# Moving low-part subtractions to GpSimd and reordering the entrance and the change of stages in a fused attention and MLP kernel

## The chip, the cores and the metric

One core of a Trainium2 chip runs the whole program. The metric is the time of one execution on the device in microseconds (us), as the median of several runs. Engines: TensorE (PE), VectorE (DVE), ScalarE (ACT), GpSimd (POOL) and SyncE (SP), whose queue issues the transfers.

## What is computed

```python
def _attn_ref(q, k, v, mem_k, mem_v):
    ...
    for c in range(nc):
        ...
        scores = scale * np.matmul(q_c, k_full.transpose(0, 1, 3, 2))
        ...
        out[:, :, c_start:c_end] = np.matmul(a, v_full)

def _moe_ref(x, w_in, w_out, g_ln):
    h = x @ w_in
    ...
    solu = h * sm
    ...
    ln = (solu - mu) / np.sqrt(var + 1e-06) * g_ln
    return (ln @ w_out).astype(np.float32)

def _moe2_ref(x, w_in, w_out):
    h = x @ w_in
    relu6 = np.clip(h + 3.0, 0.0, 6.0)
    g = h * relu6 / 6.0
    return (g @ w_out).astype(np.float32)

def reference(**kwargs):
    ...
    x = np.ascontiguousarray(attn_out.transpose(0, 2, 1, 3)).reshape(B * S, H * D)
    x = _moe_ref(x=x, **moe_kwargs)
    return _moe2_ref(x=x, **moe2_kwargs)
```

The attention is chunked (chunks of 32 queries, 16 keys to the left, 8 to the right, 8 memory keys; 4 x 8 heads of 768 x 64). x is 3072 x 512; the first MLP goes over 1024 (softmax gate, norm, `g_ln`), the second over 2048. The weights are converted to float32 and split in the kernel.

## The kernel before

The 24 tiles of 128 tokens go through attention, the first MLP's two products (`m1`, `m2`) and its norm in a loop (`BODY`). The result x2, 512 x 3072, goes to DRAM. Then follow two further stages, which are what the change is about.

**Third stage** (`mm`, L839): the product with the second MLP's `w_in`, in 6 blocks of 512 tokens and 8 units of 256 columns each, 48 units n = 8 b + u. A 2 x 2 block product is done with 7 products (the matrices' quarters are summed beforehand), and each product runs as three passes over a high and a low part of each operand: 7 x 2 x 3 = 42 matmuls of 128 x 256 a unit. VectorE puts the 7 products together (`o1` to `o4`, L866 to L878), ScalarE copies one (`p1`) and applies relu (L881), VectorE clips (`clip`, L884), and SP stores the unit to DRAM (`g_store`).

**Last stage** (`g4`, L929): the product with `w_out`, 12 groups of 256 tokens by 8 steps, again 7 products of three passes, 21 matmuls a step. A step's operand is loaded (`g_load`), summed (four `g_sum`, L914, VectorE) and split (`g_hi`, `g_lo`).

**Splitting.** Every operand tile of 128 x 512 is made into a high part (`hi_of`, L740, ScalarE) and a low part (`lo_of`, L743, VectorE: the raw tile minus the high part). There are 28 tiles of the third stage's weights (`load_w`, `w_hi`, `w_lo`; four raw tiles, halves of `qb` and `pb`), 28 of the last stage's (`load_b`, `b_hi`, `b_lo`; raw tiles `xo0`, `xo1`), of which 8 are made early, stored and fetched back (`STAGED`, `store_b`, `fetch_b`), and 7 a block of the activations (`x_hi`, `x_lo`), with four sums on GpSimd (`x_sum`, L810).

**What sets the order.** The framework keeps the order in which the program is written on each engine. Around the two stretches this is: `LAST` (L88), a table of steps for the end of the second stage, with the weights 0 to 17 prepared between the pieces of `m2`; then a loop over the units, `unit` (L1213), which spreads the rest of the weights (two a unit in units 0 to 4) and the last stage's (`b_jobs`: two a unit from unit 40 on, then one a step); and the loop over the steps (L1301), whose `get_ready` prepares the operand three steps ahead.

The core of a unit, as far as a sentence cannot say it:

```python
emit("o1", n); tail(n - 1, 0); emit("o2", n); tail(n - 1, 1); emit("o3", n)
emit("relu", n, 0); emit("p1", n + 1); low(jobs[:1])
emit("o4", n); emit("relu", n, 1); low(jobs[1:])
```

(The lines are joined here; `tail` is `clip` and, at its second call, `g_store`.)

Of the kernel before, what the change touches and what calls it, by code (L numbers as in the profile page):

```python
# [87 lines left out]
LAST = """  # L88
    m2:6,8 m2_e:6,2 m2_s:6,2 m2:6,9 m2:6,10 ln_p:23,0 ln_h:23,0 ln_l:23,0 m2:6,11 m2_e:6,3 m2_s:6,3 ln_p:23,1 ln_h:23,1
    ln_l:23,1 x_sum:0,1 x_sum:0,2 x_hi:0,5 x_lo:0,5 x_hi:0,3 x_lo:0,3 x_sum:0,4 x_hi:0,2 x_lo:0,2 x_sum:0,3  # L90
    w_hi:0 w_lo:0 load_w:4 m2:7,0 w_hi:1 w_lo:1 load_w:5 m2:7,1 w_hi:2 w_lo:2 load_w:6 m2:7,2 m2_e:7,0 m2_s:7,0 x_hi:0,6
    x_lo:0,6 x_hi:0,4 x_lo:0,4 w_hi:3 w_lo:3 load_w:7 w_hi:4 w_lo:4 load_w:8 m2:7,3 w_hi:5 w_lo:5 load_w:9 m2:7,4
    w_hi:6 w_lo:6 load_w:10 m2:7,5 m2_e:7,1 m2_s:7,1 w_hi:7 w_lo:7 load_w:11 w_hi:8 w_lo:8 load_w:12 m2:7,6 w_hi:9 w_lo:9 load_w:13
    m2:7,7 w_hi:10 w_lo:10 load_w:14 m2:7,8 m2_e:7,2 m2_s:7,2 w_hi:11 w_lo:11 load_w:15 w_hi:12 w_lo:12 load_w:16 m2:7,9
    w_hi:13 w_lo:13 load_w:17 m2:7,10 w_hi:14 w_lo:14 load_w:18 m2:7,11 m2_e:7,3 m2_s:7,3 w_hi:15 w_lo:15 load_w:19
    w_hi:16 w_lo:16 load_w:20 w_hi:17 w_lo:17 load_w:21
# [4 lines left out]
def tile_chunked_attention_solu_hardswish(  # L101
# [863 lines left out]
    with tc.manual_schedule():  # L965
# [228 lines left out]
        for entry in LAST.split():  # L1194
            run(entry)

        def tail(n, k):
            if n >= 0:
                emit("clip", n, k)
                if k:  # L1200
                    emit("g_store", n)

        b_jobs = {}
        for k, n in enumerate(STAGED):
            b_jobs[NU + NU * (k // 2) + 6 * (k % 2)] = [("b", n)]
        for n in range(11):
            b_jobs.setdefault(NU * (NX - 1) + n // 2, []).append(("b", n, 1))
        for k, n in enumerate((11, 12, 13, 18, 19, 20, 25, 26, 27)):
            b_jobs[NX * NU + k] = [("b", n, 1)]
        order = [j for n in sorted(b_jobs) for j in b_jobs[n]]  # L1210
        following = {a: b for a, b in zip(order, order[2:])}

        def unit(n, jobs):  # L1213
# [21 lines left out]
            low(late)
            if n + 1 < NX * NU:
                emit("mm", n + 1)
            i = n - NX * NU + 2
            if i == 1:
                get_ready(None, 0)  # L1240
# [11 lines left out]
            low(jobs[1:])
            if i in (-1, 0):
                get_ready(i + 1, None)
            if i == 1:
                get_ready(2, 1)
# [101 lines left out]
```

## Time and profile before

| | |
|---|---|
| median of 3 runs | 887.65 us (886.84 to 889.75) |
| the profiled execution, own time | 888.17 us |
| its span, first to last instruction | 886.4 us |
| mean granted TensorE clock | 0.994 of full |
| TensorE busy | 865.3 us (98%) |
| VectorE busy | 757.9 us (86%) |
| ScalarE busy | 467.0 us (53%) |
| GpSimd busy | 225.9 us (25%) |
| the chain that ended last | TensorE 77%, VectorE 10%, DMA 6% |

The span is that of the execution that the profiler recorded; its own time is 1.8 us longer, for what lies around the first and the last instruction. Shares are means over stages with different limits; a stretch is judged by its own rows.

### The profile page before, as it was taken

Reading aid. Unit: us, or ns where it says so; the run is one execution under the profiler, and the core shown is the slowest. Engines: PE = TensorE matmul, PEld = TensorE weight load, DVE = VectorE, ACT = ScalarE, POOL = GpSimd, SP = SyncE. Lnnn points to the kernel's source line nnn. Section 1 sums busy time; section 2 is a strip of 40 time slices with the busy share of each in tenths; the row PEclk is TensorE's granted clock in tenths of the full one; section 3 lists DMA queues with packets and bytes.
Section 4 is the critical chain, followed back from the end, with each engine's and each line's share of the span. In section 5 each row is a group of like instructions: output and inputs, shape, how many; then the busy total and the mean of one; then the engine's idle time right before and its main releaser. Section 6 shows DMA issues by size and latency. Waiting matters only on the chain.

```text
span 886.4 us, 20093 instructions
## 1 busy us (share of the span) xinstructions
PE 865.3 (98%) x7523; PEld 815.5 (92%) x7523; DVE 757.9 (86%) x1621; ACT 467.0 (53%) x865; POOL 225.9 (25%) x205
## 2 busy tenths in 40 slices
PE   9989999999999999999999999999999999999997
PEld 7777899899998989899999999999989999999997
DVE  6889987878778788677999989898899998989996
ACT  5777636566564655445545454455555444444442
POOL 4327624546455556340121111110000000000000
PEclk9999999999999999999999999999989999999999
DMA  8894347879896997438553645535786443444442
GB/s 230 213 222 113 82 128 226 237 227 300 246 269 202 290 266 230 160 121 248 194 195 147 219 153 205 195 139 209 258 268 214 147 142 122 143 139 138 142 142 73
DMA packets 184013, 168.26 MB, mean 190 GB/s; under 512 B 107116, under 2 KB 154220, under 8 KB 183916
## 3 DMA queue, kind: packets, MB, share of 16 engines
q1 hardware_dynamic: 183916, 166.98, 61.0%
q8 instruction: 59, 0.97, 0.4%
q14 instruction: 38, 0.31, 0.1%
HBM read 108.22 MB, written 58.72 MB: 188 GB/s over the span
## 4 chain that ended last, share of the span: by engine, by line
PE 77%; DVE 10%; DMA 6%; issue 3%; ACT 2%; SPq 2%; POOL 0%; DVEq 0%; ACTq 0%; POOLq 0%
PE acc L935 22%; PE acc L846 20%; PE h L556 12%; PE m L641 12%; PE tp L613 2%; PE tp L525 2%; PE sc L469 2%; DMA q_raw<-in_q_dram 1%; DMA f_pb<-sums 1%; DMA f_xo<-sums 1%; PE tp L456 1%; PE tp L507 1%; PE idle L988 1%; DMA f_xo<-w2d 1%; PE tp L441 1%
## 5 line engine op out<-in xcount | busy, mean ns | idle before, releaser
L641 PE MATMUL m<-lnh,wo 128*128 128x384 f32 x512 | 138.7, 344 | 0.0
L881 ACT ACTIVATE f_s<-f_e,constants 128x512 f32<-128x512 f32 x96 | 69.3, 722 | 96.1 <-DVE f_e L874 87.0
L556 PE MATMUL h<-w,xh 128*128 128x512 f32 x336 | 106.2, 397 | 0.1
L641 PEld LDWEIGHTS m<-lnh,wo 128*128 128x128 f32 x512 | 91.7, 189 | 0.3
L641 PE MATMUL m<-lnl,wo 128*128 128x384 f32 x256 | 88.4, 345 | 0.0
L556 PEld LDWEIGHTS h<-w,xh 128*128 128x128 f32 x336 | 61.0, 188 | 11.6 <-ACT lnh L284 0.3
L258 POOL TENSOR_SCALAR w2t<-w2t 128x512 f32<-128x512 f32 x30 | 58.4, 1946 | 51.7 <-ACT w2t L251 51.7
L884 DVE SCALAR_TENSOR_TENSOR f_s<-f_s,f_e 128x512 f32<-128x512 f32 x96 | 70.7, 737 | 0.0
L556 PE MATMUL h<-w,xl 128*128 128x512 f32 x168 | 65.7, 391 | 0.0
L245 ACT ACTIVATE kT<-tp 128x448 f32<-128x448 f32 (+3 forms) x61 | 24.7, 458 | 57.3 <-PE tp L441 49.9
L641 PEld LDWEIGHTS m<-lnl,wo 128*128 128x128 f32 x256 | 48.3, 189 | 0.0
L740 ACT ACTIVATE b_e<-f_z 128x384 fp32r<-128x384 f32 (+1 forms) x48 | 27.4, 575 | 30.0 <-DVE f_z L914 12.3
L740 ACT ACTIVATE b_qb<-f_kn 128x384 fp32r<-128x384 f32 (+1 forms) x48 | 27.1, 570 | 28.1 <-DVE f_kn L914 19.9
L245 ACT ACTIVATE qb<-tp 64x512 f32<-64x512 f32 x48 | 28.5, 594 | 18.7 <-PE tp L456 18.3
L571 ACT ACTIVATE e<-h,lst 128x1024 f32<-128x1024 f32 x24 | 26.5, 1104 | 22.2 <-DVE lst L565 22.2
L556 PEld LDWEIGHTS h<-w,xl 128*128 128x128 f32 x168 | 31.5, 188 | 6.9
L740 ACT ACTIVATE b_km<-f_q 128x384 fp32r<-128x384 f32 (+1 forms) x48 | 27.2, 570 | 19.3 <-DVE f_q L914 16.7
L878 DVE TENSOR_TENSOR f_e<-acc,f_e 128x512 f32<-128x512 f32 x48 | 32.9, 685 | 1.2
L288 DVE TENSOR_TENSOR lnl<-tp,lnh 128x512 fp32r<-128x512 f32 x41 | 26.7, 686 | 7.8 <-ACT lnh L284 7.8
L740 ACT ACTIVATE b_v<-f_xl 128x512 fp32r<-128x512 f32 x24 | 15.2, 632 | 34.4 <-DVE f_xl L914 33.6
L870 DVE TENSOR_TENSOR f_e<-acc,f_e 128x512 f32<-128x512 f32 x48 | 32.8, 683 | 0.1
L565 DVE TENSOR_REDUCE lst<-h 128x1 f32<-128x1024 f32 x24 | 29.2, 1217 | 3.5 <-PE h L556 3.4
(451 smaller groups left out, 2577.3 us busy)
## 6 DMA issues: line engine op xcount, KB each, us to landing
g<-f_s SPq DMA_DIRECT2D x48, 512.0 KB
v<-in_v_dram SPq DMA_DIRECT2D x176, 56.0 KB
w2raw<-in_moe_w_out_dram SPq DMA_DIRECT2D x16, 512.0 KB
w2raw<-in_moe_w_in_dram SPq DMA_DIRECT2D x16, 512.0 KB
w2d<-w2t SPq DMA_DIRECT2D x32, 256.0 KB
pair<-w2d SPq DMA_DIRECT2D x16, 512.0 KB
sums<-sums SPq DMA_DIRECT2D x16, 512.0 KB
q_raw<-in_q_dram SPq DMA_DIRECT2D x24, 256.0 KB
```

What stands on the lines that cost most here:

```text
L245: ACT.activation(out=out, in_=in_, func=AF.Copy)
L258: ENG[eng].tensor_scalar(out=tf, in0=tf, scalar1=U_LO, scalar2=U_HI, op0=ALU.max, op1=ALU.min)
L556: PE.matmul(h[:, f], a[:, kt], w[kt][:, f * 512:(f + 1) * 512], start=n == 0, stop=n == 3 * NKT - 1)
L565: DVE.tensor_reduce(st_t[i][:, 2:3], h_t[i].rearrange("p a b -> p (a b)"), axis=AX.X, op=ALU.max, negate=True)
L641: PE.matmul(acc, w[fc // 2][:, fc % 2, dc * P:(dc + 1) * P], a[:, fc], start=n == 0, stop=n == len(todo) - 1)
L740: ACT.activation(out=hl[0], in_=r, func=AF.Copy)
L846: PE.matmul(o, w[wl][:, c * P:(c + 1) * P], x[xl][:, c], start=m == 0 and half == 0, stop=m == 5, skip_group_check=True)
L870: DVE.tensor_tensor(c_of(n)[1], bank(n % 2, 2), wide(c_of(n)[0][:, 1]), ALU.add)
L878: DVE.tensor_tensor(c, bank(n % 2, 3), c, ALU.add)
L881: ACT.activation(out=g_of(n)[k], in_=c_of(n)[k], func=AF.Relu, bias=three, scale=1.0)
L884: DVE.scalar_tensor_tensor(out=g_of(n)[k], in0=g_of(n)[k], scalar=6.0, in1=c_of(n)[k], op0=ALU.min, op1=ALU.mult)
L935: PE.matmul(bank(t % 2, k)[:, half], g[al][:, G_BLOCK[p]], b_op[j, p][bl], start=j == 0 and m == 0 and half == 0, stop=j == NU - 1 and m = ...
```

## The change

`lo_of`, `w_lo` and `b_lo` get the engine as an argument, and 13 `w_lo` and 15 `b_lo` in the two stretches run on GpSimd. The end of the second stage and the units 0 to 9 stand in one explicit list, `LAST`; the units 39 to 47 and the steps 0 to 22 in another, `CHANGE`. In `LAST` the activations' first sum and its high part come first, and `mm:0` stands ahead of the last four pieces of `m2`. In `CHANGE` the steps run 0, 2, 1, 4, 3, 6, 5, 8, 7 and so on to 14, 13, 15. The raw tiles of `load_b` become four for 12 of the loads (two halves of `v0` beside `xo0` and `xo1`), the last stage's sums use two buffers in place of four, and the activations' homes are written out. Units 10 to 38 keep the order they had (`head`, `body`), and so do the steps from 23 on.

```diff
-    def lo_of(hl, r):
-        DVE.tensor_tensor(hl[1], r, hl[0].bitcast(F32), ALU.subtract)
+    def lo_of(hl, r, eng=DVE):
+        eng.tensor_tensor(hl[1], r, hl[0].bitcast(F32), ALU.subtract)
...
-    def w_lo(n):
+    def w_lo(n, eng=DVE):
         hl = w_halves(*W_HOME[BLOCKWISE[n]])
-        lo_of(hl, w_raw(n))
+        lo_of(hl, w_raw(n), eng)
...
+    B_RAW = ["xo0", "xo1"] * 4 + ["xo0", "xo1", "v0", "v0+"] * 3 + ["xo0", "xo1"] * 4
...
-    def b_lo(n, straight=0):
+    def b_lo(n, straight=0, eng=DVE):
         hl = b_dst(n, straight)
-        lo_of(hl, b_raw(n))
+        lo_of(hl, b_raw(n), eng)
...
-    G_RAW = (("xh", 0), ("kn0", 0), ("q0", 0), ("z1", 0))
-    G_SUM = (("xl", 0), ("kn1", 0), ("q1", 0), ("z1", 512))
-    G_HL = (("v0", "v1", 32, 0), ("qb", "pb", 32, 0), ("km", "kT", 16, 48), ("e0", "e1", 32, 0))
+    G_RAW, G_SUM = ("xh", "kn0", "pe", "z1"), ("xl", "kn1")
+    G_HL = (("km", "kT", 16, 48), ("qb", "pb", 32, 0), ("v0", "v1", 32, 0), ("e0", "e1", 32, 0))
...
 LAST = """
...
+    load_w:6 x_hi:0,4 m2:7,4 m2_s:7,0 m2:7,5 w_lo:4 x_lo:0,6 load_w:7 w_hi:6 x_lo:0,5 w_hi:5 m2_s:6,3 w_lo:6,pool
+    w_lo:5 load_w:8 m2:7,6 load_w:10 w_hi:7 m2:7,7 w_hi:8 x_lo:0,4 mm:0 p1:0 o1:0 load_w:9 w_lo:7,pool w_hi:10 w_hi:9
...
+CHANGE = """
...
+    b_lo:13,1,pool g4:0 load_b:19 g_lo:2,0 g_hi:1,1 g_load:6 o3:47 g_lo:2,1 g_lo:1,1 relu:46,0 g_hi:4,0 relu:46,1
...
+        for entry in LAST.split():
+            run(entry)
+        body(9)
+        for n in range(10, 39):
+            head(n)
+            body(n)
+        for entry in CHANGE.split():
+            run(entry)
         drains = []
-        for i, (t, j) in enumerate(G_SEQ):
-            emit("g4", i)
...
+        for i, (t, j) in list(enumerate(G_SEQ))[23:]:
+            if i > 23:
+                emit("g4", i)
             if i + 5 < len(G_SEQ):
                 emit("g_load", i + 5)
-            if i in (2, 4, 6, 8):
-                emit("fetch_b", 20 + i // 2)
...
+            get_ready(i + 3, i + 2)
```

Where the rows stand now. GpSimd from the end of the second stage on, before: the norm's last power and the first block's four sums of the activations (`f_v` is their raw tile, `f_pe` and `f_pn` the sums).

```order
L601 TENSOR_TENSOR lst<-lst,constants 128x1
L810 TENSOR_TENSOR f_pe<-f_v_4902 128x512
L810 TENSOR_TENSOR f_pn<-f_v_4904,f_pe 128x512
L810 TENSOR_TENSOR f_pe<-f_v_4904,f_pn 128x512
L810 TENSOR_TENSOR f_pn<-f_v_4904,f_v_4902 128x512
L810 TENSOR_TENSOR f_xh<-f_v_4902 128x512
L810 TENSOR_TENSOR f_xl<-f_v_4904,f_xh 128x512
```

GpSimd at the same place in the change (`b_wb`, `b_lh`, `b_wa` and so on are the weights' homes, `f_qb` and `f_pb` raw tiles):

```order
L654 TENSOR_TENSOR lst<-lst,constants 128x1
L865 TENSOR_TENSOR f_pe<-f_v_4902 128x512
L796 TENSOR_TENSOR b_wb_5085<-f_qb,b_wb_5085 128x512
L865 TENSOR_TENSOR f_pn<-f_v_4904,f_pe 128x512
L865 TENSOR_TENSOR f_pe<-f_v_4904,f_pn 128x512
L865 TENSOR_TENSOR f_pn<-f_v_4904,f_v_4902 128x512
L796 TENSOR_TENSOR b_wb_5141<-f_qb,b_wb_5141 128x512
L796 TENSOR_TENSOR b_lh_5208<-f_pb,b_lh_5208 128x512
L796 TENSOR_TENSOR b_lh_5208<-f_qb,b_lh_5208 128x512
L796 TENSOR_TENSOR b_wa_5109<-f_qb,b_wa_5109 128x512
L796 TENSOR_TENSOR b_x2r<-f_pb,b_x2r 128x512
L796 TENSOR_TENSOR b_ll_5294<-f_pb,b_ll_5294 128x512
```

One low part now stands between the first and the second sum, and twelve more follow where nothing stood.

GpSimd from the last of the activations' sums on, in the change; before, nothing follows that sum:

```order
L865 TENSOR_TENSOR f_xl<-f_v_4904,f_xh 128x512
L865 TENSOR_TENSOR f_xh<-f_v_4904,f_xl 128x512
L865 TENSOR_TENSOR f_xl<-f_v_4904,f_v_4902 128x512
L796 TENSOR_TENSOR b_wb_5085<-f_xo_5697,b_wb_5085 128x512
L796 TENSOR_TENSOR b_wb_5085<-f_xo_5808,b_wb_5085 128x512
L796 TENSOR_TENSOR b_wb_5085<-f_v_4902,b_wb_5085 128x512
L796 TENSOR_TENSOR b_wb_5141<-f_xo_5697,b_wb_5141 128x512
L796 TENSOR_TENSOR b_wo<-f_v_4902,b_wo 128x512
L796 TENSOR_TENSOR b_wb_5141<-f_xo_5808,b_wb_5141 128x512
L796 TENSOR_TENSOR b_lh_5208<-f_xo_5697,b_lh_5208 128x512
```

The low parts of the last stage's weights stand there, one after the other, 15 in all; `f_xo` and `f_v` are their raw tiles.

VectorE in the last unit of the third stage, before: `o1` to `o4` are the rows out of `acc`, L884 the clips of the unit before, L914 and L743 the sums and low parts of a step's operand.

```order
L867 TENSOR_TENSOR f_e_5456<-acc,f_pe 128x512
L884 SCALAR_TENSOR_TENSOR f_s_5402<-f_s_5402,f_e_5398 128x2x256
L870 TENSOR_TENSOR f_e_5456<-acc,f_e_5456 128x512
L884 SCALAR_TENSOR_TENSOR f_s_5402<-f_s_5402,f_e_5398 128x512
L874 TENSOR_TENSOR f_e_5456<-acc,f_e_5456 128x256
L878 TENSOR_TENSOR f_e_5456<-acc,f_e_5456 128x512
L914 TENSOR_TENSOR f_q_8040<-f_q_7840 128x128 x2
L914 TENSOR_TENSOR f_q_8040<-f_q_8040,f_q_7840 128x128
L743 TENSOR_TENSOR b_pb<-f_kn_7780,b_qb 128x384
L914 TENSOR_TENSOR f_q_8040<-f_q_7840,f_q_8040 128x128
L743 TENSOR_TENSOR b_pb<-f_kn_8020,b_qb 128x512
```

VectorE at the same place in the change (the four rows out of `acc` into `f_e_5390` are this unit's; L969 are the sums, L796 the low parts):

```order
L924 TENSOR_TENSOR f_e_5390<-acc,f_pe 128x512
L931 TENSOR_TENSOR f_e_5268<-acc,f_e_5268 128x256
L935 TENSOR_TENSOR f_e_5268<-acc,f_e_5268 128x512
L927 TENSOR_TENSOR f_e_5390<-acc,f_e_5390 128x512
L969 TENSOR_TENSOR f_xl<-f_pe 128x128
L796 TENSOR_TENSOR b_v_8043<-f_pe,b_v_8042 128x384
L931 TENSOR_TENSOR f_e_5390<-acc,f_e_5390 128x256
L796 TENSOR_TENSOR b_v_8043<-f_xl,b_v_8042 128x512
L796 TENSOR_TENSOR b_pb<-f_kn_7613,b_qb 128x512
L969 TENSOR_TENSOR f_xl<-f_xh 128x128
L969 TENSOR_TENSOR f_xl<-f_xl,f_xh 128x128
L935 TENSOR_TENSOR f_e_5390<-acc,f_e_5390 128x512
```

No clip stands there any more, and sums and low parts of three steps stand among the unit's four operations.

TensorE where the third stage begins, before: the last rows of the second stage (`m`) and the first of `mm:0`.

```order
L641 MATMUL m_5252<-lnl,wo 128x384
L641 MATMUL m_5252<-lnh,wo 128x384 x2
L641 MATMUL m_5252<-lnl,wo 128x384
L641 MATMUL m_5252<-lnh,wo 128x384
L846 MATMUL acc<-b_kn_5029,b_wb_5117 128x256
L846 MATMUL acc<-b_kn_5030,b_wb_5117 128x256
```

TensorE in the change: the last rows of `mm:0` and what follows it.

```order
L903 MATMUL acc<-b_t_5133,b_wb_5085 128x256
L903 MATMUL acc<-b_t_5132,b_wb_5085 128x256
L903 MATMUL acc<-b_z_5143,b_wa_5109 128x256 x6
L694 MATMUL m_5276<-lnh,wo 128x384
L694 MATMUL m_5276<-lnl,wo 128x384
L694 MATMUL m_5276<-lnh,wo 128x384 x2
```

Four pieces of the second stage, 32 matmuls, stand behind `mm:0` now.

## Rows read from the trace of the kernel before

**Rows 1.** Windows: length, busy us (instructions) per engine, PEclk (granted clock), DMA share, GB/s.
```profile
400.00:410.00 10.00, 10.00 (x69) 9.88 (x67) 5.90 (x10) 4.62 (x8) 0.00 (x0) 1.00 0.82 241
430.00:440.00 10.00, 9.96 (x84) 9.58 (x83) 10.00 (x18) 6.30 (x13) 0.00 (x0) 1.00 0.42 153
480.00:600.00 120.00, 120.00 (x1061) 120.00 (x1060) 108.55 (x184) 58.03 (x106) 17.84 (x13) 1.00 0.50 181
642.60:651.00 8.40, 7.08 (x35) 6.51 (x36) 8.30 (x19) 3.82 (x7) 0.00 (x0) 0.60 0.70 237
700.00:880.00 180.00, 179.77 (x1580) 179.18 (x1580) 161.81 (x480) 81.02 (x157) 0.00 (x0) 1.00 0.42 134
```

**Rows 2.** Timeline of TensorE, entrance: start, us, line, tiles, matmuls, [idle before <-releaser].
```profile
387.87 0.63 PE L613 MATMUL tp<-ident,so 128*128 128x128 f32 x4 [1.01 <-DVE so L606]
...
406.89 0.87 PE L846 MATMUL acc<-b_kn,b_wb 128*128 128x256 f32 x6
...
453.28 0.84 PE L846 MATMUL acc<-b_q,b_wb 128*128 128x256 f32 x6
453.96 0.84 PE L846 MATMUL acc<-b_km,b_wa 128*128 128x256 f32 x6
454.64 2.88 PE L846 MATMUL acc<-b_wo,b_wb 128*128 128x256 f32 x24
```

**Rows 3.** Timeline of TensorE, change of the two stages.
```profile
640.28 0.39 PE L935 MATMUL acc<-b_wb,b_v 128*128 128x256 f32 x2
642.56 2.81 PE L935 MATMUL acc<-b_wb,b_v 128*128 128x256 f32 x16 [1.90 <-DVE b_v L743]
...
647.77 0.58 PE L935 MATMUL acc<-b_wb,b_pb 128*128 128x256 f32 x1 [1.32 <-DVE b_pb L743]
...
651.68 0.39 PE L935 MATMUL acc<-b_wb,b_km 128*128 128x256 f32 x2
...
689.67 1.35 PE L935 MATMUL acc<-b_wb,b_v 128*128 128x256 f32 x9 [0.87 <-DVE f_s L946]
...
691.20 0.39 PE L935 MATMUL acc<-b_wb,b_qb 128*128 128x256 f32 x2
```

**Rows 4.** Timeline of GpSimd, same columns: sums of the activations.
```profile
384.22 1.62 POOL L810 TENSOR_TENSOR f_pn<-f_v,f_pe 128x512 f32<-128x512 f32 x1
...
424.44 1.62 POOL L810 TENSOR_TENSOR f_xl<-f_v,f_xh 128x512 f32<-128x512 f32 x1
```

**Rows 5.** Timeline of VectorE beside and away from these.
```profile
384.62 1.78 DVE L743 TENSOR_TENSOR b_q<-f_v,b_q 128x512 fp32r<-128x512 f32 x1
...
399.09 0.68 DVE L743 TENSOR_TENSOR b_wa<-f_pb,b_wa 128x512 fp32r<-128x512 f32 x1
...
424.84 0.68 DVE L878 TENSOR_TENSOR f_e<-acc,f_e 128x512 f32<-128x512 f32 x1
```

**Rows 6.** Timeline of VectorE: pace back to back, and the last unit's o4.
```profile
434.07 0.41 DVE L874 TENSOR_TENSOR f_e<-acc,f_e 128x256 f32<-128x256 f32 x1
434.41 0.68 DVE L743 TENSOR_TENSOR b_wo<-f_qb,b_wo 128x512 fp32r<-128x512 f32 x1
435.01 0.68 DVE L878 TENSOR_TENSOR f_e<-acc,f_e 128x512 f32<-128x512 f32 x1
...
645.95 0.69 DVE L878 TENSOR_TENSOR f_e<-acc,f_e 128x512 f32<-128x512 f32 x1
...
654.72 0.49 DVE L914 TENSOR_TENSOR f_kn<-f_kn 128x128 f32<-128x128 f32 x2
...
656.64 0.69 DVE L743 TENSOR_TENSOR b_ll<-f_xo,b_ll 128x512 fp32r<-128x512 f32 x1
```

**Rows 7.** Groups of VectorE from 453 to 640: busy us, mean ns | idle before.
```profile
L884 DVE SCALAR_TENSOR_TENSOR f_s<-f_s,f_e 128x512 f32<-128x512 f32 x80 | 58.9, 737 | 0.0
```

**Rows 8.** Chain of waits at the entrance: start, us, what.
```profile
396.92 2.81 DMA f_pb<-sums
...
406.23 3.99 DMA f_pb<-sums
```

More of the change, by code (lines that the diff above doesn't have):

```diff
@@ L88 @@
 LAST = """
[L89 to L93, printed above, removed]
@@ new lines @@
+    w_lo:23 load_w:24 o1:4 o2:4 clip:3,0 load_w:25 w_hi:24 w_hi:25 w_lo:24 o3:4 load_w:27 p1:5 w_hi:27 o1:5 clip:3,1
+    o4:4 x_hi:1,3 w_lo:22,pool load_w:26 o2:5 g_store:2 w_hi:26 x_lo:1,3 mm:6 p1:6 w_lo:26 x_hi:1,2 o3:5 o4:5
+    w_lo:25,pool load_b:14 w_lo:27,pool relu:4,0 relu:4,1 clip:4,0 clip:4,1 x_lo:1,1 x_lo:1,2 o1:6 o2:6 o3:6 x_sum:1,4
+    x_sum:1,3 mm:7 p1:7 x_hi:1,5 x_lo:1,5 x_hi:1,4 x_lo:1,4 o4:6 x_hi:1,6 x_lo:1,6 mm:8 g_store:3 relu:5,0 relu:5,1
+    clip:5,0 clip:5,1 load_b:15 g_store:4 load_x:2 relu:6,0 o1:7 relu:6,1 p1:8 o2:7 o3:7 o4:7 mm:9 p1:9 clip:6,0 o1:8
@@ L812, in x_hl @@
     def x_hl(b, i):
-        return [t.rearrange("p (k t) -> p k t", k=2) for t in halves(*X_HOME[(7 * b + i) % len(X_HOME)])]
+        tag = X_HOME[b][i]
+        where = ("wo", int(tag[2]), 16) if tag[:2] == "wo" else ((tag + "0", tag + "1"),) if tag in ("kn", "q", "t") else (tag,)
+        return [t.rearrange("p (k t) -> p k t", k=2) for t in halves(*where)]
     def x_hi(b, i):
@@ L898, in g_tile @@
     def g_tile(i, which):
-        tag, o = which[i % 4]
-        return home(tag, F32)[:, o:o + 512].rearrange("p (b t) -> p b t", t=P)
+        return home(which[i % len(which)], F32)[:, 0:512].rearrange("p (b t) -> p b t", t=P)
     def g_hl(i):
@@ L1192, in emit, with head @@
             run(name + ":" + ",".join(map(str, args)))
[L1194 to L1213, printed above, removed]
+        def head(n):
             b, u = divmod(n, NU)
-            late = []
             if b + 1 < NX:
@@ L1235, in unit, with taken_over @@
[L1235 to L1240, printed above, removed]
+            for kind, *a in taken_over(n) + jobs(n):
+                emit(kind + "_hi", *a)
+            for kind, *a in taken_over(n):
+                emit(kind + "_lo", *a)
+            emit("mm", n + 1)
+        def taken_over(n):
+            b, u = divmod(n, NU)
+            return [("x", b + 1, i) for i in (4, 5, 6)] if u == 7 else []
@@ L1246, in unit @@
             emit("relu", n, 0)
-            if n + 1 < NX * NU:
-                emit("p1", n + 1)
-            low(jobs[:1])
+            emit("p1", n + 1)
+            for kind, *a in jobs(n)[:1]:
+                emit(kind + "_lo", *a)
             emit("o4", n)
             emit("relu", n, 1)
[L1252 to L1256, printed above, removed]
-            for job in mine:
-                if job in following:
-                    emit("load_b", following[job][1])
-                if len(job) == 2:
-                    emit("store_b", job[1])
@@ L1262, in unit @@
-            if b + 1 < NX and u in (4, 5):
+            for kind, *a in jobs(n)[1:]:
+                emit(kind + "_lo", *a)
+            for kind, *a in jobs(n):
+                if kind == "b":
+                    emit("load_b", B_ORDER[B_ORDER.index(a[0]) + 2])
+                    emit("store_b", *a)
+            if u in (4, 5):
                 emit("x_sum", b + 1, 8 - u)
```

116 lines of the change are left out of this document (64 added, 52 removed).

## The prediction

> **What bounds the kernel now.** I read the windows of busy time first, to find the stretches in which TensorE is not full. In long stretches it is: 120.00 of 120 us between 480 and 600, 179.77 of 180 between 700 and 880 [rows 1]. There nothing can be won by moving work between other engines. What is left are the two stretches that the change rewrites, and there I read TensorE's timeline against its own pace. At full clock a product of six matmuls starts 0.68 us after the one before (453.28 to 453.96), so a unit of third-stage work (`mm`, seven products) takes 4.76 us and a step of the last stage (`g4`, 21 matmuls) half of that, 2.38 us [rows 2].
>
> The entrance: `mm:0` starts at 406.89, `mm:9` at 454.64. That is 47.75 us for nine units that need 9 x 4.76 = 42.84, so 4.9 us are lost. Ahead of it TensorE waits 1.01 us at 387.87 for the `so` tile of VectorE [rows 2]. Together 5.9 us.
>
> The change of stages: `g4:0` starts at 640.28 and the 18th step at 691.20. 50.92 us for 17 steps that need 40.46: 10.5 us are lost [rows 3]. Of these 1.90, 1.32 and 0.87 are waits for VectorE (642.56, 647.77, 689.67). The rest of the stretch from 642.56 to 651.68 holds 40 matmuls, 4.53 us at pace, and takes 9.12; without the 1.32 of waiting that is 3.3 us too many, and the granted clock there is 0.60 of the full 2.4 GHz, most of it at the 1.2 GHz level [rows 1, 3]. It fell after the wait of 1.90 us; after those of 1.01 and 0.87 us it did not [rows 2, 3]. The remaining 3.1 us are small waits for VectorE.
>
> So at most 16.4 us can be won, 1.8% of the time, all of it on the path: TensorE's lost time is the program's.
>
> **The change, part by part.** The work is the same, matmul for matmul; what moves are the orders, and 13 `w_lo` and 15 `b_lo` from VectorE to GpSimd.
>
> *VectorE's load.* Back to back, a 512-element operation there costs 0.60 us and the 256-element one 0.34 (434.07, 434.41, 435.01), and getting one `g4` step ready (four sums of about 0.20, two low parts of 0.47 and 0.60) 1.92 (654.72 to 656.64) [rows 6]. So a unit (`o1` to `o4`, two clips) costs 5 x 0.60 + 0.34 = 3.34 of its 4.76 us, and a last-stage step 1.92 of 2.38. Before, units 40 to 45 carried two `b_lo` each but the last (4.54 us), and steps 0 to 8 one each (2.52, over TensorE's 2.38): this is why VectorE came late at 640 and stayed late. The 15 moved `b_lo` take 15 x 0.60 = 9.0 us off it in this stretch, and the 13 `w_lo` 7.8 us off the entrance.
>
> Adding the durations in the new order, with 1.2 us for two of the three activations' low parts ahead of `mm:40` as still running when it starts: by the end of `mm:47`, 38.1 us later, VectorE has 32.5 us of work to do (42 operations of 0.60, 8 of 0.34, 12 of 0.20, 2 of 0.47, and the 1.2); by `g4:9`, at 61.9, it has 56.8; by `g4:13`, at 71.4, 66.9. The spare is 5.6, 5.1 and 4.5 us; I take the smallest. In the entrance 49.7 us of VectorE work stand before `mm:10` at 70.7: a spare of 21 us.
>
> *What GpSimd takes back.* The cover of the moved subtractions is a GpSimd that stood idle; its 15 need at most 15 x 1.62 = 24.3 us of the 40 they have. They are not free. While GpSimd subtracted for 1.62 us at 384.22, a VectorE subtraction between two SBUF tiles took 1.78 us (384.62) and not 0.68 (399.09); one that reads PSUM kept its 0.68 (424.84) beside the GpSimd operation of 424.44 [rows 4, 5]. The worst price is thus 1.10 us of VectorE time for each moved operation. The least: between 453 and 640 the 80 clips average 737 ns where 680 is undisturbed, as for the 0.68 of the other 512-element operations [rows 6, 7]: 80 x 0.057 = 4.6 us for the 16 GpSimd sums there, 0.28 us each. Of VectorE's work from `mm:40` to `g4:2`, 20.7 of 39.3 us reads two SBUF tiles, which gives 0.53 x 1.10 = 0.58. I take 0.45, between 0.28 and 0.58. The change then loses 15 x 0.45 = 6.75 us of VectorE against a spare of 4.5: 2.25 us of waiting for TensorE. In the entrance, 20 GpSimd operations cost 9 us, hidden by the 21.
>
> The Trainium skill, in SBUF — State Buffer, Who interferes with whom, says that a VectorE instruction with two SBUF inputs contends with a GpSimd instruction that reads SBUF, that whoever is first holds the shared pair for its whole instruction, and that one with at most one SBUF input does not contend. The 1.78 and the 0.68 agree with it; by the rule alone the sum would go with 1.10 for each, and that is the first rival.
>
> *The order at the entrance.* `mm:0` moves ahead of four second-stage pieces, so the products that wait for weights come with filler behind `mm:0`. Its inputs were ready at 399.8, with the `w_lo` of 399.09, for a start at 406.89 [rows 2, 5]; the new start is 5.6 us earlier, leaving 1.5 us. The second sum of the activations moves behind a `w_lo` on GpSimd, so it no longer runs beside the subtraction of 1.78 us that held up `so`: that wait of 1.01 us goes. What I leave is 1.5 us, a quarter of the loss, because weight loads of 2.8 to 4.0 us stay on the chain [rows 8] with the same four raw tiles. Gain 5.9 - 1.5 = 4.4 us.
>
> *The order at the change.* `g4` now runs 0, 2, 1, 4, 3, so each pair of steps uses one set of weights and later sets are due one step later; the low parts of step 0 stand ahead of `mm:47`'s results. With no wait of 1.9 us the 3.3 us at the lower clock go too. What stays is the 2.25 us and half of the 3.1 us of small waits, 1.5, which a sum of loads cannot see. Gain 10.5 - 3.75 = 6.7 us.
>
> *Queues.* On GpSimd each `b_lo` waits for its load and its high part, and the next ones wait behind it; `g4` of their set waits for them; sets 1 to 7 are due one step, 2.4 us, later than before. The sums of the activations now stand behind `w_lo`s there. On SP the stores of units 46 and 47 move behind later loads; they are read in the last block of steps only, so nobody waits.
>
> *Cheap edits.* Two more raw tiles for `load_b` (`v0` in halves), two sum buffers in place of four in the last stage (both users are VectorE, in order) and the new homes of the activations add no instruction, and VectorE's 1.92 in 2.38 us hides a late tile; without that cover it is a small wait as now. Units 10 to 38 keep their order: nothing.
>
> **Sum.** 4.4 + 6.7 = 11.1 us off the profiled execution's 888.17 gives 877.1; the median of the runs is 0.5 below that execution, so 876.5.
>
> **The rivals.** *GpSimd takes all back (slower).* Place: VectorE between `mm:43` and `g4:9`. At 1.10 us each, 16.5 us against 4.5 of spare: 12.0 us of waiting, 1.5 of small ones, and the clock falls as at 642 (3.3): 16.8 lost where 10.5 are lost now. In the entrance 20 x 1.10 = 22 us use up the spare of 21, and nothing is won. 888.17 + 6.3 - 0.5 = 894. For it: 384.62. Against it: the PSUM rows and the 0.28. With the clock's fall it decides from 15c - 4.5 + 1.5 + 3.3 = 10.5, c about 0.7 us for each; about that price, with nothing won in the entrance, the time stays at 887 to 888, no change.
>
> *Weights come late at the entrance.* The chain there is load, high part, low part [rows 8], and a low part on GpSimd holds its raw tile up to 0.9 us longer. Then only the 1.01 us is won there: 888.17 - 1.0 - 6.7 - 0.5 = 880. For it: VectorE stands idle for 4.1 of 10 us at 400 to 410, in this chain. Against it: at 430 to 440, where TensorE loses time, VectorE is full, 10.00 of 10 us [rows 1].
>
> *The bank of `g4:2`.* It writes the banks of unit 47, is now second, and needs the last one 2.38 + 5 x 0.34 = 4.1 us after `mm:47`. Now `o4:47` ends at 646.64, 6.4 us after it [rows 3, 6]. If that stays so, 2.3 us of waiting and the clock's 3.3 come back: 10.5 - 9.3 = 1.2 won there, 882 in all. Against it: the new order has no `b_lo` there, and two low parts and two sums between `o3:47` and `o4:47`, 1.6 us.
>
> **How the numbers follow.** Forecast 0.58; late weights 0.12; the bank 0.08; GpSimd's price near 0.7 us 0.09; in full 0.13. A run of this kernel tells about 0.3%, 2.7 us, from no change. Faster: 0.58 + 0.12 + 0.08 = 0.78; same 0.09; slower 0.13. Low end: all 16.4 us go, 871.3, and a little stays: 872. High end: it takes in 880, 882 and half of the no-change case, 887; left out are 0.13, half of 0.09 and a little below.
>
> **What would show it.** Right: no wait at the 387.87 place; `mm:0` to `mm:9` with its four second-stage pieces within 1.5 us of pace; `g4` steps without a wait over 1 us and a granted clock of 1.00 from 600 to 700; VectorE subtractions of 1.2 to 1.8 us beside GpSimd's, 15 x 0.45 us in all. Wrong: TensorE waiting for `b_lo` or `w_lo` on GpSimd, a clock below 1.00 after `mm:47`, or a lengthening of VectorE over 10 us in the change.

## The result, and the profile after

The changed kernel takes **879.25 us** (median of 4 runs, 878.19 to 881.52) against 887.45 us (4 runs, 886.84 to 889.75) of the kernel before in the same comparison: ratio 0.9906, 95% interval 0.988 to 0.9933. It is faster, by 8.2 us. The profiled execution took 878.19 us, its span is 876.4 us and its mean granted clock 1.00.

The two profiled executions differ by 9.98 us (888.17 and 878.19). Cut at the same five places of TensorE's work, they differ like this (us; the starts come from TensorE's timelines, each column behind the first is the time from the place ahead of it):

| | start of the last `ln_p` | to `mm:10` | to `g4:0` | to the 18th step | to the end |
|---|---|---|---|---|---|
| before | 387.87 | 71.53 | 180.88 | 50.92 | 195.16 |
| after | 387.84 | 66.63 | 180.88 | 42.77 | 198.26 |
| difference | -0.03 | -4.90 | 0 | -8.15 | **+3.10** |

The first column says little: in the executions of this study it lies between 385.0 and 389.6 us, mostly in code that no kernel changes. The middle one is 180.88 wherever the units 10 to 47 were left alone and fed. So both rewritten stretches won, and the last stage, of which the prediction expected nothing, lost 3.1 us.

Windows of the kernel after (length, busy us (instructions) of TensorE, its weight loads, VectorE, ScalarE, GpSimd, then granted clock, DMA share, GB/s), for [rows 1]:

```profile
400.00:410.00 10.00, 10.00 (x74) 10.00 (x73) 7.07 (x12) 5.61 (x10) 4.18 (x4) 1.00 0.65 196
430.00:440.00 10.00, 10.00 (x91) 10.00 (x90) 9.04 (x16) 6.37 (x12) 6.06 (x4) 1.00 0.79 254
480.00:600.00 120.00, 120.00 (x1062) 120.00 (x1061) 108.47 (x185) 58.81 (x109) 16.23 (x12) 1.00 0.51 187
637.00:645.00 8.00, 7.71 (x65) 7.46 (x65) 7.97 (x21) 5.93 (x12) 0.00 (x0) 1.00 0.84 273
700.00:860.00 160.00, 158.45 (x1377) 157.06 (x1376) 146.30 (x424) 71.19 (x138) 0.00 (x0) 1.00 0.42 133
```

At 430 TensorE is full where VectorE was full before, the clock after `g4:0` is 1.00 where it was 0.60, and the last stage has 1.55 us of 160 in which TensorE isn't busy; before it was 0.23 of 180.

TensorE's timeline after, at the places of [rows 2, 3]: the last `ln_p`, `mm:0`, `mm:10`, `g4:0`, the two waits of the change, the 18th step (start, us, line, tiles, matmuls, [idle before <-releaser]):

```profile
387.84 1.06 PE L666 MATMUL tp<-ident,so 128*128 128x128 f32 x8
...
401.23 0.86 PE L903 MATMUL acc<-b_km,b_wb 128*128 128x256 f32 x6
...
454.47 0.73 PE L903 MATMUL acc<-b_wo,b_lh 128*128 128x256 f32 x5
...
635.35 0.39 PE L990 MATMUL acc<-b_wb,b_km 128*128 128x256 f32 x2
...
640.04 0.62 PE L990 MATMUL acc<-b_wb,b_v 128*128 128x256 f32 x3 [0.29 <-DVE f_e L935]
...
667.56 0.86 PE L990 MATMUL acc<-b_ll,b_e 128*128 128x256 f32 x5 [0.54 <-DMA b_ll<-b_d]
...
678.12 0.39 PE L990 MATMUL acc<-b_wb,b_qb 128*128 128x256 f32 x2
```

The wait of 1.01 us at the last `ln_p` is gone and TensorE waits for nothing up to `mm:10`. In the change 42.77 us stand against 40.46 at pace: 2.3 us lost where 10.5 were. About 1.1 of the 2.3 are lost at the fetch of finished weights (667.56) and 0.6 at 640.04, where TensorE waits for VectorE to empty a bank.

VectorE in the last stage, after, two neighbouring steps, for [rows 6]:

```profile
810.90 0.69 DVE L796 TENSOR_TENSOR b_kT<-f_xl,b_km 128x512 fp32r<-128x512 f32 x1
811.62 0.49 DVE L969 TENSOR_TENSOR f_xl<-f_pe 128x128 f32<-128x128 f32 x2
...
813.62 0.49 DVE L969 TENSOR_TENSOR f_kn<-f_z 128x128 f32<-128x128 f32 x2
```

A step costs VectorE 2.00 us now (811.62 to 813.62); the same stretch of the kernel before shows 1.88:

```profile
822.57 0.49 DVE L914 TENSOR_TENSOR f_q<-f_q 128x128 f32<-128x128 f32 x2
...
824.45 0.69 DVE L914 TENSOR_TENSOR f_z<-f_z 128x128 f32<-128x128 f32 x3
```

The 0.12 us stand between the low part at 810.90 and the sum at 811.62: with two sum buffers that sum writes the tile (`f_xl`) which the low part just ahead of it reads, and starts 0.72 us after it instead of 0.60. VectorE then has little left at the end of each block of eight steps, where it also drains the accumulators, and TensorE waits there (page of waits after, 690 to 872 us):

```profile
PE acc L990 <- DVE b_v L796: 0.8, 2, 0.6
PE acc L990 <- DVE b_kT L796: 0.7, 4, 0.2
```

Beside GpSimd, VectorE's lengthenings in the change are few. The 15 `b_lo` at 600 to 637 us cost it 2.8 us together (each operation less its undisturbed duration, added up from the timeline), 0.19 us each. The dearest of them, and an operation that reads `acc` while GpSimd runs as well (a `b_lo` from 627.26 to 629.03):

```profile
626.04 1.82 DVE L796 TENSOR_TENSOR b_kT<-f_xl,b_km 128x512 fp32r<-128x512 f32 x1
...
628.30 0.69 DVE L935 TENSOR_TENSOR f_e<-acc,f_e 128x512 f32<-128x512 f32 x1
```

### The profile page after: what moved, and what is told of

The parts are those of the page before. It is cut to its first block, busy times and chain, and to the rows that moved or that the text cites. A ratio compares the mean times of both kernels' runs of the same rounds, so it can differ in the third digit from the quotient of the medians.

```text
span 876.4 us, 20127 instructions
## 1 busy us (share of the span) xinstructions
PE 859.8 (98%) x7523; PEld 811.8 (93%) x7523; DVE 749.3 (86%) x1593; ACT 466.8 (53%) x865; POOL 263.9 (30%) x233
## 4 chain that ended last, share of the span: by engine, by line
PE 80%; DVE 9%; DMA 5%; issue 2%; ACT 2%; SPq 2%; POOL 0%; ACTq 0%; DVEq 0%; POOLq 0%
PE acc L903 25%; PE acc L990 20%; PE m L694 14%; PE h L609 12%; PE tp L666 2%; PE tp L578 2%; PE sc L522 2%; DMA q_raw<-in_q_dram 1%; DVE f_s L1001 1%; PE tp L560 1%; PE tp L509 1%; DVE f_xl L969 1%; DMA w1raw<-in_moe_w_in_dram 1%; DVE f_kn L969 1%; PE tp L494 1%
## 5 line engine op out<-in xcount | busy, mean ns | idle before, releaser
L793 ACT ACTIVATE b_km<-f_xl 128x512 fp32r<-128x512 f32 x26 | 16.4, 631 | 34.2 <-DVE f_xl L969 26.6
L644 ACT ACTIVATE e<-so,lst 128x1024 f32<-128x1024 f32 x24 | 27.4, 1143 | 7.6 <-DVE lst L640 7.6
L635 DVE SCALAR_TENSOR_TENSOR so<-h,lst,e 128x1024 f32<-128x1024 f32 x24 | 30.7, 1278 | 0.5
```

What stands on the lines that cost most here:

```text
L635: DVE.scalar_tensor_tensor(out=so_t[i], in0=h_t.pop(i).rearrange("p a b -> p (a b)"), scalar=st[:, 5:6], in1=e_t[i], op0=ALU.mult, op1=ALU ...
L793: ACT.activation(out=hl[0], in_=r, func=AF.Copy)
```

## The experiments

Each ran on one chip with the kernel before, and its ratio is to that kernel's runs there (medians 886.49, 889.21 and 888.53 us on the three chips). The columns of the stage table are named: "entrance" is last `ln_p` to `mm:10`, "change" is `g4:0` to the 18th step, "last stage" is the rest.

**1. Four sum buffers again.** The changed kernel, one edit:

```diff
 def g_tile(i, which):
+    if which is G_SUM and i >= 8:
+        tag, o = (("xl", 0), ("kn1", 0), ("q1", 0), ("z1", 512))[i % 4]
+        return home(tag, F32)[:, o:o + 512].rearrange("p (b t) -> p b t", t=P)
```

> The changed kernel with four sum buffers in place of two from step 8 on; nothing else. Theory: in the changed kernel each step of the last stage costs VectorE 2.00 us and not 1.88, because a step's first sum writes the buffer that the low part just ahead of it on VectorE reads, and must wait for its end; at each group's end this makes TensorE wait, 2.7 us in all after 700. With four buffers the step is 1.88 us again, TensorE's waits at each group's end go, and the time is 876 to 877.5. Rival: the waits come from the transfers or from the order of the results' sums; then the step stays at 2.00 us or the waits stay, and the time is 878.5 to 879.5 as in the changed kernel.

Measured: 873.38 us (4 runs, 872.57 to 874.06), ratio 0.985 (0.9828 to 0.9873). VectorE's timeline:

```profile
802.44 0.68 DVE L796 TENSOR_TENSOR b_v<-f_q,b_v 128x512 fp32r<-128x512 f32 x1
803.04 0.49 DVE L972 TENSOR_TENSOR f_xl<-f_xh 128x128 f32<-128x128 f32 x2
...
804.92 0.49 DVE L972 TENSOR_TENSOR f_kn<-f_kn 128x128 f32<-128x128 f32 x2
```

The sum follows after 0.60 us again, a step costs 1.88, the page of waits lists none of TensorE's in the last stage, and that takes 193.44 us. The stretch gained 4.8 us, more than the 2.7 that the theory counted, and the time is 2.6 us below the range expected. All kernels of this study with two sum buffers show 196.2 to 198.6 there, all undisturbed ones with four 193.4 to 195.2. So the "cheap edit" of the sum buffers is what lost the 3.1 us. In this profile the change took 45.73 us, not 42.77: a fetch of finished weights came late there (run 8).

**2. The orders without GpSimd**: every `,pool` taken out of the two tables (`w_lo:0,pool` to `w_lo:0`, and so on).

> The changed kernel's orders with all 28 moved low parts back on VectorE. Theory: GpSimd's relief is what makes the change of stages fit. VectorE gets 14 to 15 x 0.60 = 8.4 to 9.0 us more there against a spare of 4.5, so TensorE waits 4 to 8 us around the first steps of the last stage, with a granted clock under 1.00 if one wait is near 2 us; in the entrance 7.8 us stay inside the spare of 21 and nothing or at most 1 us is lost. Time 884 to 888. Rival: the orders alone bring the gain and GpSimd is of no account, since it takes back what it gives; then 878 to 880.

Measured: 890.55 us (10 runs, 887.44 to 894.75), ratio 1.0049 (1.0028 to 1.007). Entrance 74.06 us (71.53 before, 66.63 after), change 48.65. It is 2.6 us above the range expected, which allowed the entrance a loss of 1 us. The largest waits of TensorE in the two stretches, in their order of time:

```profile
PE acc L903 <- DVE b_ll L796: 2.4, 1, 2.4
...
PE acc L990 <- DVE f_e L931: 2.3, 1, 2.3
```

Both are VectorE coming late: first with a low part of the weights, then with `o3:46`, which empties a bank that `g4:0` writes. The wait for `so` is back too, 1.00 us at 384.98: with `w_lo:0` off GpSimd the second sum of the activations starts early again, and beside it a VectorE subtraction takes 1.78 us (381.73); in the changed kernel that subtraction takes 0.68 (385.69). The new orders by themselves don't win; the last stage of this kernel, with its two sum buffers, holds 1.9 us of the time (197.08 against 195.16).

**3. GpSimd without the orders**: the kernel before, with the same 28 low parts on GpSimd.

```diff
-        lo_of(hl, w_raw(n))
+        lo_of(hl, w_raw(n), POOL if n in (0, 6, 7, 8, 10, 13, 15, 17, 18, 19, 22, 25, 27) else DVE)
...
-        lo_of(hl, b_raw(n))
+        lo_of(hl, b_raw(n), POOL if straight and n in tuple(range(14)) + (18,) else DVE)
```

> The kernel before, with every order as it was, and only the engine changed: the same 13 low parts of the first weights and 15 of the second go to GpSimd. With the run that has the new orders and no GpSimd this completes the four combinations. Theory (VectorE's load is what bounds the change of the stages, and GpSimd alone takes most of that off): g4's first 17 steps in 45 to 47 us instead of 50.9; at the entrance, where the order itself puts the weights late, little: 70 to 71.5; in all 882 to 884 us. Rival (the orders and the move need each other, since in the old order GpSimd's operations stand beside two-SBUF work and hold it up): 49 us or more in the change, 886 us or more in all.

Measured: 894.67 us (10 runs, 891.03 to 899.66), ratio 1.0072 (1.0047 to 1.0097), the slowest kernel here: the theory falls, and the rival's times hold. Entrance 72.91, change 53.38. Windows, of it and then of the kernel before:

```profile
600.00:640.00 40.00, 40.00 (x355) 40.00 (x354) 30.58 (x50) 20.47 (x39) 14.63 (x11) 1.00 0.62 207
```
```profile
600.00:640.00 40.00, 40.00 (x355) 40.00 (x355) 35.70 (x65) 20.95 (x39) 0.00 (x0) 1.00 0.66 226
```

VectorE was relieved, 30.58 us of work in the 40 ahead of the change and not 35.70, and stood idle instead. GpSimd, SP's queue, ScalarE and VectorE of the same kernel show why:

```profile
620.45 2.72 POOL L743 TENSOR_TENSOR b_wb<-f_xo,b_wb 128x512 fp32r<-128x512 f32 x2 [2.42 <-ACT b_wb L740]
```
```profile
623.20 0.52 SPq L729 DMA_DIRECT2D f_xo<-w2d  x1
```
```profile
627.61 0.64 ACT L740 ACTIVATE b_lh<-f_xo 128x512 fp32r<-128x512 f32 x1 [1.78 <-DMA f_xo<-w2d]
...
628.77 0.36 ACT L864 ACTIVATE f_e<-acc 128x256 f32<-128x256 f32 x1
```
```profile
629.16 0.69 DVE L867 TENSOR_TENSOR f_e<-acc,f_e 128x512 f32<-128x512 f32 x1 [2.83 <-ACT f_e L864]
```

The second of GpSimd's two low parts ends at 623.17 and frees one of the two raw tiles; the next load is issued at 623.20; ScalarE waits for it with a high part at 627.61; `p1` stands behind that in ScalarE's order, and `o1` on VectorE waits 2.83 us for `p1`. The longer low part holds the raw tile longer, and the chain of load, high part and low part runs slower, through three in-order queues. Where VectorE does catch up it meets GpSimd, and `g4:0` waits longer than in [rows 3]. GpSimd, VectorE and TensorE at the change:

```profile
638.26 1.30 POOL L743 TENSOR_TENSOR b_wa<-f_xo,b_wa 128x512 fp32r<-128x512 f32 x1 [4.02 <-ACT b_wa L740]
```
```profile
638.43 1.27 DVE L914 TENSOR_TENSOR f_xl<-f_xh,f_xl 128x128 f32<-128x128 f32 x1
```
```profile
644.69 3.78 PE L935 MATMUL acc<-b_wb,b_v 128*128 128x256 f32 x16 [3.39 <-DVE b_v L743]
```

The rival's mechanism has a part in it: the same 15 `b_lo` cost VectorE 7.1 us here, 0.47 each, against 2.8 us in the new order (added up from the timelines in the same way).

Runs 2 and 3 with the two kernels make four corners: neither 1, orders (with the cheap edits) 1.0049, GpSimd 1.0072, both 0.9906. Each part alone gains nothing, though the corner with the orders carries the loss of the two sum buffers, and the one with GpSimd has only two raw tiles. In the changed kernel `load_b` has four raw tiles and ScalarE's longest wait for one between 600 and 635 us is 1.66 us (631.41), behind which `p1` still waits for TensorE; how much of that is the two more raw tiles and how much the order wasn't tried.

**4. Old entrance, new change.** The changed kernel with the entrance's table and unit loop of before.

```diff
-        for entry in LAST.split():            # new table, up to mm:10
+        for entry in OLD_LAST.split():        # table of before, up to mm:0
             run(entry)
+        emit("mm", 0)
+        emit("p1", 0)
+        for n in range(0, 10):
+            old_unit(n)
```

> The changed kernel with the entrance (the end of the second stage and units 0 to 9) in the order of before, all on VectorE; the change of stages as changed. Theory: the entrance is worth its 5.9 us by itself, so the time is 884 to 885.5, with the waits of 1 us for so and the losses from 410 to 455 as before, and 640 to 690 as in the changed kernel. Rival: the entrance's gain is given back later, since VectorE's backlog only moves; then 879 to 880.5.

Measured: 882.95 us (10 runs, 880.87 to 890.41), ratio 0.9968 (0.9945 to 0.999). Entrance 72.06 us as before (71.53), change 44.57 near the changed kernel's 42.77, last stage 196.16 with its two sum buffers. The time lies 1 us below the theory's range and 2.4 above the rival's; the stages show that the change of stages doesn't need the new entrance.

**5. New entrance, old change**, twice. First with the new homes of the activations in the kernel before:

```diff
-    X_HOME = [(("kn0", "kn1"),), (("q0", "q1"),), ("km",), ...]
+    X_HOME = [block.split() for block in ("km kT kn q z1 t z0", "wo4 wo5 wo6 wo7 km kT kn", ...)]
```

> The kernel before with the entrance as changed (13 low parts on GpSimd, mm:0 ahead of the last four pieces); the change of stages and the last stage as before. Theory: the parts add, so 887.5 - 5.9 = 881 to 882.5, with the waits of 1.9 and 1.3 us and the clock of 0.60 at the start of the last stage as before, and no waits at the ends of groups in the last stage. Rival: without relief at the change the entrance's gain is lost there, 886 to 888.

Measured: 890.55 us (10 runs, 887.17 to 892.64), ratio 1.004 (1.0019 to 1.0061). The entrance took 67.35 us, but 8.1 us were lost between `mm:10` and `g4:0`:

```profile
PE acc L859 <- DVE f_e L891: 6.5, 1, 6.5
```

This says nothing on the entrance: the cut was wrong. The new homes put activations of the last block into `q`, and the old change of stages loads its raw tiles of the last stage there; one waits for the other. The homes belong to both stretches. Again with the homes of before:

> The kernel before with the changed entrance alone (its order, its low parts on GpSimd), this time with the activations' homes of before, so that the change of the stages is untouched. Theory (the two stretches are independent and add up): ln_p:23 to mm:10 in 66.6 to 67.4 us instead of 71.5, g4's first 17 steps in 50 to 51 as before, in all 881.5 to 883 us. Rival (what the entrance wins is lost again later, because VectorE arrives at the same point with the same work): 885 to 887.

Measured: 881.73 us (7 runs, 877.58 to 886.4), ratio 0.9928 (0.9897 to 0.9959). Entrance 66.63, the same as in the changed kernel to the hundredth; change 50.27, last stage 194.48, as the theory had it. So the two stretches are independent: 0.7% come from the entrance here, 0.3% from the change in run 4, where the two sum buffers take as much away.

**6. The filler ahead of `mm:0`.** In the changed kernel:

```diff
-    m2:7,6 ... m2:7,7 ... mm:0 p1:0 ... m2_e:7,1 m2:7,9 ... m2:7,8 ... m2:7,10 ... m2:7,11 ... mm:1
+    m2:7,6 ... m2:7,7 ... m2:7,8 m2_e:7,1 m2:7,9 m2:7,10 m2:7,11 mm:0 p1:0 ... mm:1
```

> The changed kernel with the four second-stage pieces put ahead of mm:0 again; the low parts stay on GpSimd. Theory (the filler behind mm:0 is what the products use while weights are still being split): mm:0 starts some 5 us later, and the products behind it then wait for weights, for 2 to 4 us in all: 881 to 883 us. Rival (relieving VectorE alone did it, and the place of the filler is indifferent): no wait over 0.3 us at the entrance, the same 66.6 us from ln_p:23 to mm:10, and 879 to 879.5 us.

Measured: 884.13 us (10 runs, 880.7 to 887.04), ratio 0.9954 (0.9937 to 0.9971). Entrance 70.97: 4.3 us lost, but TensorE's only wait is not for weights:

```profile
415.22 1.65 PE L903 MATMUL acc<-b_q,b_wb 128*128 128x256 f32 x6 [2.72 <-DVE x2o L699]
416.67 1.48 PE L903 MATMUL acc<-b_z,b_wb 128*128 128x256 f32 x6
```

`mm:1` uses the second stage's accumulators, and the copies that empty them (`m2_e`) stood behind unit 0's clips on VectorE. Products after that wait take 1.28 us (416.67 to 417.95), not 0.68, and the granted clock of 410 to 420 is 0.83: the rest of the 4.3 us. With these copies moved ahead too:

> As the run with the four second-stage pieces ahead of mm:0, but the three copies that empty the second stage's accumulators (m2_e:7,1 to 7,3) are moved ahead with them, so that mm:1 no longer waits for these. Theory (there the 4.3 us were lost on the accumulators alone, 2.7 of waiting and the rest at the lower clock, not on weights): from ln_p:23 to mm:10 66.6 to 67.5 us, 878 to 880 us in all. Rival (the filler behind mm:0 is needed, since the weights of mm:1 and mm:2 are split behind o1 to o4 of unit 0, which come 4 us later): a wait for low parts of weights of 1 us or more, 69 us or more, 882 us or more.

Measured: 885.5 us (10 runs, 881.57 to 889.78), ratio 0.9972 (0.9946 to 0.9997), entrance 74.15. VectorE and TensorE:

```profile
411.56 0.56 DVE L699 COPY x2o<-m 128x384 f32<-128x384 f32 x1 [10.28 <-DMA x2d<-x2o]
```
```profile
422.87 1.65 PE L903 MATMUL acc<-b_km,b_ll 128*128 128x256 f32 x6 [3.43 <-DVE f_e L924]
```

The third copy now waits 10.28 us for its buffer, whose store stands on SP behind a weight load that in turn waits for GpSimd, and everything behind it on VectorE is late. The theory falls; the rival's times hold, but TensorE's long wait is not for a low part. What these two runs show is that the place of the four pieces hangs together with copies, stores and loads on two queues; whether weights alone would be late without the filler isn't separated by them and stays open.

**7. The price of a GpSimd operation.** The kernel of run 1 with 32 extra 128x512 additions on GpSimd whose results are not read: in units 16 to 23 behind a clip (the clip's result plus weights), in units 26 to 33 behind `o4` (its result plus weights), in steps 48 to 63 as soon as the raw tile is there (raw tile plus itself).

```diff
+            if 16 <= n < 24: emit("extra_unit", n - 1, 1)
...
+            if 26 <= n < 34: emit("extra_unit", n, 0)
...
+            if 48 <= i < 64: emit("extra_step", i + 3) 
```

> The kernel with four sum buffers and extra 128x512 subtractions' equals on GpSimd whose results nobody reads: one in each of units 16 to 23, started when a clip ends (next on VectorE: operations that read PSUM); one in each of units 26 to 33, started when o4 ends (next but one on VectorE: a clip, two SBUF inputs); one in each of steps 48 to 63 of the last stage, where nearly all of VectorE's work has two SBUF inputs. Theory (the price is set by the two-SBUF work that stands beside, one whole instruction held up at most): 0.1 to 0.3 us of VectorE each in the first place, 0.5 to 1.0 in the second, 1.0 to 1.6 in the third, where a step then costs VectorE 2.9 to 3.4 us instead of 1.88 against TensorE's 2.38, so that TensorE loses 0.5 to 1.0 us in each of the 16 steps: 881 to 889 us. Rival (the average of 0.45 holds anywhere): 2.3 us per step, nothing lost, 873 to 874 us.

Measured: 888.03 us (10 runs, 887.29 to 891.18), ratio 0.9996 (0.9979 to 1.0012); the middle stage 185.21 us (4.3 more), the last 204.64 (about 10 more). GpSimd's timeline, one operation for each case:

```profile
496.48 1.30 POOL L986 TENSOR_TENSOR f_pe<-f_s,b_wb 128x512 f32<-128x512 f32 x1 [3.69 <-DVE f_s L941]
...
505.92 1.31 POOL L986 TENSOR_TENSOR f_pe<-f_s,b_wb 128x512 f32<-128x512 f32 x1 [1.99 <-DVE f_s L941]
...
543.21 1.32 POOL L986 TENSOR_TENSOR f_pe<-f_e,b_wb 128x512 f32<-128x512 f32 x1 [7.47 <-DVE f_e L935]
...
780.67 1.20 POOL L991 TENSOR_TENSOR f_t<-f_xh 128x512 f32<-128x512 f32 x1 [1.52 <-DMA f_xh<-g]
...
801.36 6.89 POOL L991 TENSOR_TENSOR f_t<-f_pe 128x512 f32<-128x512 f32 x1 [2.28 <-DMA f_pe<-g]
```

and VectorE beside each of them:

```profile
496.78 0.69 DVE L935 TENSOR_TENSOR f_e<-acc,f_e 128x512 f32<-128x512 f32 x1
...
506.03 1.74 DVE L796 TENSOR_TENSOR b_kT<-f_v,b_kT 128x512 fp32r<-128x512 f32 x1
...
543.58 1.49 DVE L941 SCALAR_TENSOR_TENSOR f_s<-f_s,f_e 128x512 f32<-128x512 f32 x1
...
780.89 1.53 DVE L972 TENSOR_TENSOR f_z<-f_z 128x128 f32<-128x128 f32 x3
```

PSUM is the memory of TensorE's accumulators (`acc`); the raw tiles, the parts and the sums lie in SBUF. An operation that reads PSUM isn't touched (0.69). One with two SBUF inputs that is issued while GpSimd runs ends 0.54 us after GpSimd does, where it takes 0.68 alone: 506.03 ends at 507.77, GpSimd at 507.23; 543.58 at 545.07, GpSimd at 544.53. So the price is about the rest of GpSimd's operation: 1.0 us at once behind its start, 0.8 a little later, 0.45 later still (571.15 and 580.20), nothing beside PSUM. In the last stage 12 of the first 15 cost VectorE 0.84 to 0.85 us, the other three nothing. My expectation for the first place (0.1 to 0.3 us) was wrong for 6 of its 8, where a low part follows `o3` and took the full 1.0 us. That there is an average of 0.45 that holds anywhere is excluded. Part of the last stage's loss came by another way, loads of raw tiles that came late (VectorE waits 3.4 us for them between 750 and 830), likely because GpSimd held the tiles longer.

**8. The late fetch.** Run 1 with `fetch_b:23` directly behind `fetch_b:16` in the table of the change:

```diff
-    ... g_hi:13,1 fetch_b:23 g_sum:16,1 ...
+    ... fetch_b:16 fetch_b:23 load_b:25 ...
```

> The kernel with four sum buffers, and one fetch of finished weights (fetch_b:23) issued on SP behind fetch_b:16, ahead of the loads of raw tiles that wait for VectorE. Theory (what is left in the change of stages is this late fetch and the clock's fall after it): the stretch from g4's first step to its 18th goes from 45.7 us to 42 to 43, the last stage stays at 193.5, and the kernel takes 870 to 871 us. Rival (the transfer itself is slow, 7 us wherever it starts, or it only pushes another one late): the stretch stays at 45 to 46 and the time at 873.

Measured: 873.76 us (6 runs, 870.26 to 876.34), ratio 0.9832 (0.9805 to 0.9858). Change 42.61 us; the wait is gone that in run 1 was

```profile
PE acc L993 <- DMA b_ll<-b_d: 1.8, 2, 1.6
```

That the time would be 870 to 871 us was missed on a chip where the kernel before took 889.21. Both once more on one chip:

> The kernel with four sum buffers again, on the same chip as the one with the earlier fetch, for their difference: 0.985 of the kernel before.

> The kernel with four sum buffers and the earlier fetch again, beside the one without: theory 2 to 3 us less (0.982 of the kernel before), as its change of stages was 3.1 us shorter in the profile; rival: the same within 1 us, because the late fetch costs only in some executions.

Measured: without 874.19 us (5 runs, 873.08 to 876.13), 0.9836 (0.9809 to 0.9863); with 872.6 us (6 runs, 870.3 to 873.35), 0.9809 (0.9782 to 0.9837). In these profiles the change takes 43.32 and 43.17 us. The late fetch cost 3 us in the first profile, where the granted clock fell behind the wait (0.79 from 665 to 673), and next to nothing in this one, where TensorE waits 1.1 us for it in two pieces and the clock stays at 1.00. That is the rival's reason; the medians differ by 1.6 us, between the rival's 1 and the theory's 2 to 3. The two intervals overlap; a gain is likely, not settled. Either kernel beats the changed one and the one before; the best of this study is the changed kernel with four sum buffers and the earlier fetch, 1.7 to 1.9% under the kernel before.

## Why the prediction came out as it did

The forecast of 876.5 us was 2.75 us low; the result lies in the range of 872 to 887, on the forecast side. Its sum was 4.4 + 6.7 = 11.1 us; the profiles give 4.90 + 8.15 - 3.10 = 9.95, and with 0.03 ahead of the entrance 9.98. Errors cancelled in it: the two gains came out 1.95 us larger than forecast, and the last stage lost 3.1 that the sum didn't have, which leaves 1.1 us of the miss. The other 1.6 us are the runs': the forecast put the median some 0.6 us below the profiled execution, and the changed kernel's lies 1.06 above it. That 876.5 came so near is in part luck.

- **Entrance, forecast 4.4.** The stretch won 4.9 us and the wait of 1.01 us went as well, though in this execution unchanged code ahead of it took as much longer. The 1.5 us that I left over were not lost at all, seven of the eight profiles with this entrance show 66.63 us. Run 5 shows the stretch standing alone.
- **Change, forecast 6.7.** 8.2 us were won. The clock's fall went with the wait, as said. 2.3 us are left where I left 3.75, and of another kind: the 2.25 us of waiting that GpSimd's price was to cost did not come, since 2.8 us of price stay within the spare of 4.5, and the fetch and the bank make most of the 2.3. That 2.3 lies so near to 2.25 is luck.
- **GpSimd's price, 0.45 us: mis-sized and of the wrong kind.** It measured 0.19 in the change, and 0.47 for the same operations in the old order (run 3). The bounds of 0.28 and 0.58 were averages over work that had two-SBUF operations beside it; the 15 `b_lo` of the new order mostly stand beside `o1` to `o4`, which read PSUM. Run 7 shows a price from 0 to 1.05, by what is issued beside it and when. The rule of the Trainium skill, SBUF — State Buffer, Who interferes with whom, that two SBUF inputs contend with GpSimd and at most one does not, fits this, and the trace agrees: 0.69 beside PSUM, 1.74 with two SBUF inputs. What I did wrong was to weigh it by share of time where the order decides.
- **That VectorE's load is why it came late at 640: failed as the one cause.** Run 3 took that load away and the change got longer, 53.38 us: VectorE idled behind the chain of loads, through ScalarE. The forecast held since the change moves the orders and the raw tiles too.
- **The entrance's "spare of 21 us": failed.** Run 2 puts the 13 `w_lo` back, 7.8 us of the 21, and loses 7.4 us. A spare summed over a stretch hides nothing if the work is due inside it: the longest wait there is for one low part, 2.4 us, others add 2.0, and the granted clock falls to 0.94 and 0.89 in the 20 us from 430.
- **"Cheap edits: nothing": failed.** It said that both users of a sum buffer are VectorE, in order, and that the 1.92 in 2.38 us hides what is late. In order is not for free: a write behind a read of the same tile costs 0.12 us of overlap in each step. The spare of 0.46 us a step covers it, but not where the drains of a block stand too. It cost 3.1 us between the two profiles, and run 1 wins 4.8 back.
- **The rivals.** GpSimd taking all back didn't happen; run 3 comes to its time, 894.67 against 894, but in part only by its mechanism: the 15 cost VectorE 0.47 us each there and not 1.10, and the chain of loads is longer. Late weights and the bank of `g4:2` didn't happen: no wait at the entrance, 0.29 us at 640.04 for the bank. In the signs to look for, TensorE waiting on low parts made by GpSimd didn't show; a wait for a DMA of finished weights, 0.54 us, which I had not counted under queues, did, and reached 1.8 us in run 1.
